# A routed mixture of experts behind a gated scan: how the first pages of tokens are cut and handed on

## The chip, the cores and the metric

The kernel runs on one core of one Trainium2 chip. The metric is the device time of one execution in microseconds. TensorE (PE in the profile, PEld its weight loads) does the matmuls, VectorE (DVE) and ScalarE (ACT) the elementwise work, GpSimd (POOL) starts the scatters, and SyncE (SP) starts the loads.

## The reference

There are 4 sequences of 5056 steps with 256 channels. A gated linear scan runs along each; its 20224 outputs are tokens. Each token goes to the one of 8 experts with the largest logit, passes two layers of that expert, and is scaled by its gate.

```python
for t in range(S):
    h = a_t[:, t] * h + x_gated[:, t]
    y[:, t] = h
...
logits = x @ w_gate + modality_bias[modality_id]
e_idx = np.argmax(logits, axis=1)
...
for e in range(E):
    mask = e_idx == e
    h = np.maximum(x[mask] @ w1[e], 0.0)
    out[mask] = gate_w[mask, None] * (h @ w2[e])
```

The gate's logits are small beside the bias of the token's modality, and there are two modalities, drawn at random. So nearly all tokens go to two experts, which the kernel calls hot.

## The kernel before, in words

**Chunks.** The steps are cut into 23 chunks: four of 128 steps (512 tokens over the 4 sequences), seventeen of 256 (1024 tokens), one of 128 and one of 64. For each chunk the kernel loads its inputs (`load_chunk`), runs the scan on VectorE (`scan_chunk`), scales and splits the result into two halves of 16 bits (`size_chunk`, `split_chunk`), routes it (`route_chunk`) and scatters its rows to a list in memory (`rows_part`, `scatter`, L813). In the list each expert has a region of its own of NCAP rows; a token's place is the expert's region plus its running count. `route_chunk` keeps the running counts in `be`, and those of the two hot experts, in units of 256 rows, in a small tile `b2` for each chunk (L800).

**Pages.** Work for TensorE comes in pages: that many consecutive rows of one expert's region. `choose_pages` runs along with everything else, and `choose_two` makes a pair, one page of each hot expert. It writes the first rows of the two pages to a tile `sel` (L917), which SyncE reads into a register before it loads the rows (`load_rows`: a transposing load of X at L1091, and the gates `mt` at L1092). `u` holds how far each hot expert has been handed on. The size of a pair is fixed when the program is built, while the counts are known only on the chip. So a pair is handed on when the tokens routed so far, less a margin `behind` for each hot expert, cover all that was chosen plus the new pair. If an expert has fewer rows than the page needs, its `sel` is set to `NULLS`, a page of null rows whose outputs go nowhere, and `u` stays.

The first pair has 128 rows per page, the next ones 256, and after the weights' block sums are ready (`block_sums`) pairs of 512 (`WIDE`), whose first layer takes 14 groups of products instead of 16. When all is routed, one pair of 256 that need not be full ends the hot list.

**Cold pages.** What is left goes to pages of 128 of whichever expert has most left (`choose_cold`). Such a page loads that expert's two weights, 1 MB each, through four buffers `wr` (`cold_weights`), scales and converts them into halves on ScalarE and VectorE (L297, L347, L350, L353) and then runs as other pages do. One is chosen for the experts that are not hot, one at the very end for any. Then `over` is the largest count still left (L984). If it is 1 or more, a block of instructions behind a branch (`more_pages`, L1401) chooses and runs two more such pages, and inside it a further branch does the same with six, and so on.

**Order.** A planner in the kernel's own code (`run`) decides the order of the instructions on each engine when the program is built: each thread yields an engine, a duration and a condition, and the earliest, or of near ones the most urgent, is issued. `mark`, `room` and `give` are its due times and buffers. `drained(n)` is the time at which TensorE has begun pages of n rows in all; `look` holds choices back to 384 rows ahead of that, or 2944 once the block sums are there. On the chip the engines follow the order and wait for each other by semaphores only.

TensorE interleaves a page's first layer (L1166, or L1256 for pages of 512) with the second layer of the page before (L1326). A page's hidden values pass ScalarE and VectorE (L1103, L1105), its outputs ScalarE (L1117), and a scatter on GpSimd (L1121) puts 128 rows at a time into the result.

Of the kernel before, what the change touches and what calls it, by code (L numbers as in the profile page):

```python
# [9 lines left out]
F32 = mybir.dt.float32  # L10
# [4 lines left out]
ALU = mybir.AluOpType  # L15
AX = mybir.AxisListType

P = 128
B, S, D, E, FF = 4, 5056, 256, 8, 1024
# [3 lines left out]
WIDE = 512  # L23
NCAP = N + 256
NULLS = E * NCAP
# [4 lines left out]
CHUNKS = [(128 * k, 128) for k in range(4)] + [(512 + 256 * k, 256) for k in range(17)] + [(4864, 128), (4992, 64)]  # L30
# [4 lines left out]
HOT = 2  # L35
# [11 lines left out]
C_STEP = 2  # L47
URGENT = 0.5
HURRY = 5
ROW_STEP = 2.4  # L50
LAG = 3.0


def behind(n):

    return 1.2 * n ** 0.5 + 8


def columns(c):
# [18 lines left out]
def kernel(  # L78
# [13 lines left out]
    nc = tc.nc  # L92
    pool = lambda name, bufs, **k: ctx.enter_context(tc.tile_pool(name=name, bufs=bufs, **k))
    const = pool("const", 1)
    pa = pool("pa", 2)
    sm = pool("sm", 2)
# [30 lines left out]
    for e in range(E):  # L127
# [23 lines left out]
        out=cmp, in0=rank.rearrange("p e o -> p o e").broadcast_to(one8), in1=ids.broadcast_to(one8), op=ALU.is_equal  # L151
# [7 lines left out]

    u = const.tile([1, HOT], F32, name="u")  # L160
    nc.vector.tensor_scalar(out=u, in0=key[:, 0:HOT, 0], scalar1=NCAP / 256.0, scalar2=None, op0=ALU.mult)
    cold = const.tile([1, E], F32, name="cold")
    nc.vector.tensor_scalar(out=cold, in0=ev, scalar1=HOT - 0.5, scalar2=8.0, op0=ALU.is_ge, op1=ALU.mult)

# [16 lines left out]
        out=um1, in_=um1, pattern=[[1, P]], base=0, channel_multiplier=-1,  # L181
# [33 lines left out]
    plan = {"end": 0.0}  # L215
# [4 lines left out]
    def room(tag, k=1):  # L220

        def at():
            d = slots[tag]
            old = [n - d.bufs for n in range(d.n, d.n + k) if n >= d.bufs]
            return max((d.back.get(n, FAR) for n in old), default=0.0)
        return at
# [8 lines left out]
    def allof(*fs):  # L235
        def at():
            t = 0.0
            for f in fs:
                t = max(t, f())
                if t >= FAR:  # L240
                    break
            return t
        return at
# [446 lines left out]
    def rows_part(c, j):  # L690
# [34 lines left out]
        for u in range(k):  # L725
            yield "POOL", ROW_STEP if c > 7 else 1.3, None
            scatter(f"rows{c}", rt[:, u, 0:ROW], di[:, PART * j + u : PART * j + u + 1])
# [84 lines left out]
    def scatter(group, src, idx):  # L812
        ins = nc.gpsimd.indirect_dma_start(  # L813
            out=rows[:, :], out_offset=bass.IndirectOffsetOnAxis(ap=idx, axis=0),
            in_=src, in_offset=None, bounds_check=NULLS + WIDE - 1, oob_is_err=False,
        ).ins
        for gname in written:
            tc.declare_no_dep(ins, group=gname, reason="every token has a row of its own")
        tc.declare_no_dep(ins, group="loads", reason="a page's rows are written before it is chosen")
        if group not in written:  # L820
            written.append(group)
        puts.append((group, ins.name))
        tc.add_to_no_dep_group(group, ins)
        free["DMA"] = max(free["DMA"], plan["end"] - 1.3) + 0.37
        if "pe" in count:

            tc.add_manual_dep(
                ins, count["pe"], mybir.DependencyInfo(mybir.DependencyClass.Sync, mybir.DependencyReason.DATA)
            )
# [7 lines left out]
    def null_rows():  # L837

        for k in range(2):
# [3 lines left out]
            for e in range(E):  # L843
                yield "POOL", ROW_STEP, None
                scatter("rows_null", nt, ni[:, e : e + 1])
# [13 lines left out]
    pages, queue = [], []  # L859
    count = {"chosen": 0, "ended": False, "cold": 0, "rows": 0}  # L860
# [3 lines left out]
    def routed(t=FAR):  # L864
        n = 0
        while n < NC and all(mark.get(("put", n, j), FAR) <= t for j in range(parts(n))):
            n += 1
        return n

    def enough():  # L870

        at, have = 0.0, 0
        want = count["chosen"] + HOT * (256 if pages else P)
        for c in range(NC):
            at = max([at] + [mark.get(("put", c, j), FAR) for j in range(parts(c))])
            if at >= FAR:
                return FAR
            have += B * CHUNKS[c][1]
            if have - HOT * behind(have) >= want:
                return at  # L880
        return at

# [20 lines left out]
        if not left:  # L903
            give("sel", ticket)

    def choose_two(size, full):

        sel, ticket = new_sel()
        b2 = tiles["b2", routed(plan["end"]) - 1]
        z = size / 256  # L910
        if full:
            d = sm.tile([1, HOT], F32, name=f"d{len(pages)}", tag="d2")
            nc.vector.tensor_tensor(out=d, in0=b2, in1=u, op=ALU.subtract)
            yield "DVE", 0.08, None, 0.0
            nc.vector.tensor_scalar(out=d, in0=d, scalar1=z, scalar2=float(NULLS), op0=ALU.is_lt, op1=ALU.mult)
            yield "DVE", 0.08, None, 0.0
            nc.vector.scalar_tensor_tensor(out=sel, in0=u, scalar=256.0, in1=d, op0=ALU.mult, op1=ALU.max)  # L917
            first = plan["end"]
            yield "DVE", 0.08, None, 0.0
            if z == 1:  # L920
                nc.vector.scalar_tensor_tensor(out=u, in0=d, scalar=0.0, in1=u, op0=ALU.is_equal, op1=ALU.add)
            else:
                nc.vector.tensor_scalar(out=d, in0=d, scalar1=0.0, scalar2=z, op0=ALU.is_equal, op1=ALU.mult)
                yield "DVE", 0.08, None, 0.0
                nc.vector.tensor_tensor(out=u, in0=u, in1=d, op=ALU.add)
        else:
            nc.vector.tensor_scalar(out=sel, in0=u, scalar1=256.0, scalar2=None, op0=ALU.mult)
            yield "DVE", 0.08, None, 0.0
            nc.vector.scalar_tensor_tensor(out=u, in0=u, scalar=z, in1=b2, op0=ALU.add, op1=ALU.min)
        left = [0] * HOT  # L930
        for e in range(HOT):
            pg = new_page(size, e, sel, e, not full)
            pg.ticket = ticket, left
            queue_page(pg)
        count["chosen"] += HOT * size
# [51 lines left out]
    def choose_pages():  # L987
        other, at = None, FAR
        summed = lambda: max(mark.get(("sw", e), FAR) for e in range(HOT))
        look = lambda: drained(count["chosen"] - (LOOK if summed() >= FAR else LOOK_END))()  # L990
        while True:
            yield "DVE", 0.08, allof(enough, room("sel"), look)
            if other is None and routed(plan["end"]) == NC:

                add(null_rows(), (0, 5), plan["end"])
                other, at = (yield from choose_cold(True)), len(pages) + 2 * HOT
                add(cold_weights(other), (1, 3), plan["end"])
                yield "DVE", 0.08, room("sel")
            if len(pages) >= at:
                queue_page(other)  # L1000
                at = FAR
            have = sum(B * t for _, t in CHUNKS[: routed(plan["end"])])
            size = 256 if pages else P
            if summed() <= plan["end"] and have - HOT * behind(have) >= count["chosen"] + HOT * WIDE:
                size = WIDE
            if have - HOT * behind(have) < count["chosen"] + HOT * size:
                break
            yield from choose_two(size, True)
        yield "DVE", 0.08, allof(room("sel"), look, seen("null"))
        yield from choose_two(256, False)  # L1010
        if at < FAR:
            queue_page(other)

        t = sm.tile([1, HOT, E], F32, name="thot", tag="thot", bufs=1)
        yield "DVE", 0.08, None, 0.0
        for r in range(HOT):
            nc.vector.tensor_scalar(out=t[:, r], in0=hm[:, r], scalar1=u[:, r : r + 1], scalar2=65536.0, op0=ALU.mult, op1=ALU.mult)
        for r in range(HOT):
            nc.vector.tensor_tensor(out=tk, in0=tk, in1=t[:, r], op=ALU.max)

        yield "DVE", 0.08, room("sel")
        last = yield from choose_cold(False)
        queue_page(last)
        add(cold_weights(last), (1, 3), plan["end"])
        tiles["over"] = over()
        count["ended"] = True
# [342 lines left out]
    def start_chunk(c):  # L1369
        at = PRIO.get(c, (9 + C_STEP * c, 10 + C_STEP * c, 11 + C_STEP * c, 10 + C_STEP * c))  # L1370
        add(load_chunk(c), (0, 10 + C_STEP * c))
        add(scan_chunk(c), (0, at[2]), urgent=c < HURRY)
        add(size_chunk(c), (0, at[2]), urgent=c < HURRY)
        add(split_chunk(c), (0, at[1]), urgent=c < HURRY)
        add(route_chunk(c), (0, at[0]), urgent=c < HURRY)
        for j in range(parts(c)):
            add(rows_part(c, j), (1, at[3]), urgent=c < HURRY)

# [83 lines left out]
```

## Time and profile before

| what | value |
|---|---|
| median of three runs | 951.44 us (950.36 to 954.1) |
| the profiled execution | 952.39 us, of which the span of the profile is 950.5 us |
| mean granted TensorE clock | 0.978 |
| PE busy | 869.7 us, 91% of the span |
| DVE, ACT, POOL busy | 700.0, 671.6, 484.7 us |
| moved by the DMA queues | 160.43 MB, mean 169 GB/s |

The page gives busy time for each engine, then the span in 40 equal slices with the busy share in tenths, the granted clock and the DMA share. A row of a group names the line, engine, operation, what it writes and reads, how many, the busy time and mean, and after the bar the idle time ahead of it with what ended it. A row of a timeline begins with the start and the length in us. A row of a stage has its bounds, its length, then for each engine the busy time with the number of instructions, the granted clock, the DMA share and GB/s.

### The profile page before, as it was taken

How to read it: one execution, taken by the hardware profiler on the slowest of the kernel's cores; microseconds unless marked ns; L12 is line 12 of the kernel's file. 1: busy time of each engine (PE TensorE's matmuls, PEld its weight loads, DVE VectorE, ACT ScalarE, POOL GpSimd, SP SyncE). 2: the span in 40 equal slices, each digit the busy share in tenths (PEclk: the TensorE clock that was granted, in tenths of full speed). 3: DMA queues.
4: the chain of work that ended last, by engine and by line, in shares of the span. 5: the costliest groups of instructions: out<-in, count | busy, mean ns of one | idle time of the engine just before them, and what ended most of it. 6: DMA issues, size and time to landing. Idle time of an engine off the chain costs nothing.

```text
span 950.5 us, 22224 instructions
## 1 busy us (share of the span) xinstructions
PE 869.7 (91%) x8462; PEld 775.0 (82%) x8462; DVE 700.0 (74%) x1535; ACT 671.6 (71%) x960; POOL 484.7 (51%) x506
## 2 busy tenths in 40 slices
PE   2268995879999999999999999999999999999996
PEld 1256884769898888888888888988888888888886
DVE  4977785788888877799886888976886666645551
ACT  6876795866898778889578789844765555554742
POOL 5232456367876758857776658745544221222122
PEclk9988997989999999999999999999999999999999
DMA  8746896759999799987788988685733322213410
GB/s 292 230 150 175 223 244 166 223 135 221 267 203 228 226 256 232 265 224 195 185 217 185 274 208 214 163 161 119 184 79 85 57 62 51 52 45 68 131 36 24
DMA packets 222759, 160.43 MB, mean 169 GB/s; under 512 B 197297, under 2 KB 201522, under 8 KB 216114
## 3 DMA queue, kind: packets, MB, share of 16 engines
q1 hardware_dynamic: 205714, 114.49, 51.2%
q0 software_dynamic: 16224, 44.25, 14.2%
q8 instruction: 68, 1.11, 0.5%
q14 instruction: 49, 0.40, 0.1%
q10 hardware_dynamic: 704, 0.18, 0.1%
HBM read 72.96 MB, written 44.48 MB: 124 GB/s over the span
## 4 chain that ended last, share of the span: by engine, by line
PE 46%; issue 21%; DVE 11%; DMA 8%; POOL 7%; ACT 6%; POOLq 0%; SPq 0%; ACTq 0%; DVEq 0%
PE po L1326 21%; PE ph L1166 21%; POOL out_dram L1121 5%; DMA rows<-rt,di 3%; DVE x L546 3%; DVE H L1105 2%; DMA X<-rows 2%; DMA rt<-a 2%; POOL rows L813 1%; PE pb L1256 1%; DVE x L531 1%; ACT H L1103 1%; PE psl L679 1%; PE pa L1256 1%; DVE g L517 1%
## 5 line engine op out<-in xcount | busy, mean ns | idle before, releaser
L1166 PE MATMUL ph<-X,hw 128*128 128x256 f16 (+1 forms) x2688 | 332.1, 276 | 27.3 <-DMA X<-rows 27.3
L1326 PE MATMUL po<-hw,H 128*128 128x256 f16 x2640 | 328.1, 274 | 2.9 <-DVE H L1105 2.7
L1121 POOL DMA_INDIRECT out_dram<-ot,mt x160 | 195.3, 1221 | 259.7 <-ACT ot L1117 217.9
L813 POOL DMA_INDIRECT rows<-rt,di x158 | 229.4, 1452 | 173.3 <-issue 40.7
L1166 PEld LDWEIGHTS <-hw 128*128 128x128 f16 x2688 | 261.3, 100 | 59.5 <-DMA X<-rows 21.3
L1326 PEld LDWEIGHTS <-H 128*128 128x128 f16 x2688 | 259.5, 98 | 35.0 <-DVE H L1105 3.5
L1105 DVE SCALAR_TENSOR_TENSOR H<-ph,H 128x512 f16<-128x512 f32 (+1 forms) x232 | 151.8, 665 | 80.0 <-ACT H L1103 79.6
L1103 ACT ACTIVATE H<-ph 128x512 f16<-128x512 f32 (+1 forms) x232 | 133.2, 578 | 99.9 <-PE ph L1166 88.1
L1117 ACT ACTIVATE ot<-po,gt 128x256 f32<-128x256 f32 x160 | 75.2, 471 | 50.5 <-PE po L1326 43.5
L546 DVE TENSOR_TENSOR_SCAN x<-a,x 128x2048 f32<-128x2048 f32 (+2 forms) x23 | 88.1, 3829 | 0.8
L1326 PE MATMUL po<-hw,Hx 128*128 128x256 f16 x576 | 81.8, 273 | 0.1
L1326 PE MATMUL po<-hw,Hg 128*128 128x256 f16 x576 | 80.2, 273 | 0.0
L1326 PEld LDWEIGHTS <-Hx 128*128 128x128 f16 x576 | 56.2, 98 | 6.7 <-issue 0.3
L1326 PEld LDWEIGHTS <-Hg 128*128 128x128 f16 x576 | 56.4, 98 | 6.5
L1256 PEld LDWEIGHTS <-sw 128*128 128x128 f16 x576 | 56.4, 98 | 6.5
L531 DVE TENSOR_TENSOR x<-g,x 128x2048 f32<-128x2048 f32 (+2 forms) x23 | 45.8, 1991 | 15.8 <-ACT x L529 15.8
L663 ACT ACTIVATE a<-x,scy 128x1024 f16<-128x1024 f32 (+2 forms) x46 | 45.8, 1021 | 12.3 <-DVE scy L289 12.3
L666 DVE SCALAR_TENSOR_TENSOR a<-x,scy,a 128x1024 f16<-128x1024 f32 (+2 forms) x46 | 50.8, 1122 | 1.7 <-ACT a L663 1.7
L522 ACT ACTIVATE a<-a,ch 128x1024 f32<-128x1024 f32 (+2 forms) x46 | 50.7, 1118 | 0.0
L1103 ACT ACTIVATE Hg<-sv 128x512 f16<-128x512 f32 x48 | 30.0, 627 | 26.5 <-DVE sv L1204 26.2
L517 DVE SCALAR_TENSOR_TENSOR g<-g,x 128x2048 f32<-128x2048 f32 (+2 forms) x23 | 45.6, 1984 | 2.9 <-ACT g L513 2.9
L1199 ACT ACTIVATE sv<-pb 128x512 f32<-128x512 f32 x48 | 28.6, 595 | 25.9 <-PE pb L1256 24.3
(210 smaller groups left out, 1109.2 us busy)
## 6 DMA issues: line engine op xcount, KB each, us to landing
a<-in_r_gate_dram SPq DMA_DIRECT2D x17, 1024.0 KB
g<-in_i_gate_dram SPq DMA_DIRECT2D x17, 1024.0 KB
x<-in_x_dram SPq DMA_DIRECT2D x17, 1024.0 KB
wr<-in_moe_w_dram SPq DMA_DIRECT2D x4, 1024.0 KB
cr<-in_moe_w_dram SPq DMA_DIRECT2D x4, 1024.0 KB
a<-in_r_gate_dram SPq DMA_DIRECT2D x5, 512.0 KB
g<-in_i_gate_dram SPq DMA_DIRECT2D x5, 512.0 KB
x<-in_x_dram SPq DMA_DIRECT2D x5, 512.0 KB
```

Source lines behind the costliest of these rows:

```text
L517: nc.vector.scalar_tensor_tensor(out=g, in0=g, scalar=1.0, in1=x, op0=ALU.add, op1=ALU.mult)
L531: nc.vector.tensor_tensor(out=y, in0=g, in1=y, op=ALU.mult)
L546: nc.vector.tensor_tensor_scan(out=y, data0=a, data1=y, initial=0.0, op0=ALU.mult, op1=ALU.add)
L666: nc.vector.scalar_tensor_tensor(out=ys[:, 1, :, u, :], in0=yg[:, :, u, :], scalar=sc, in1=ys[:, 0, :, u, :], op0=ALU.mult, op1=ALU.subtract,)
L813: ins = nc.gpsimd.indirect_dma_start(out=rows[:, :], out_offset=bass.IndirectOffsetOnAxis(ap=idx, axis=0), in_=src, in_offset=None, bounds ...
L1103: nc.scalar.activation(hi, src, AF.Relu)
L1105: nc.vector.scalar_tensor_tensor(out=lo, in0=src, scalar=0.0, in1=hi, op0=ALU.max, op1=ALU.subtract)
L1117: nc.scalar.activation(ot, po, AF.Copy, scale=t.gt[:, a : a + 1])
L1121: ins = nc.gpsimd.indirect_dma_start(out=out[:, :], out_offset=bass.IndirectOffsetOnAxis(ap=t.mt[:, a, 0:1], axis=0), in_=ot, in_offset=No ...
L1166: ins = nc.tensor.matmul(ph[:, v, 0:st], lhsT, rhs, start=(m == 0 and v == 0), stop=(m == len(mm) - 1), skip_group_check=True,)
L1256: ins = nc.tensor.matmul(to[:, v, :], lhsT[s], rhs[x], start=(i in (1, 7) and v == 0 and m == 0), stop=(m == 2), skip_group_check=True,)
L1326: ins = nc.tensor.matmul(prev.po, prev.h(hx, f, rs_), wv[:, wx, f], start=(prev.count == 1), stop=(prev.count == 3 * NF))
```

## The change

The margin `behind` becomes 0 for the chunks 0 to 5 and stays as it was from chunk 6 on. The first pair has 256 rows per page like the following ones. While at most six chunks are routed, `choose_two` takes a new form: a page begins at `u`, or where fewer than 256 new rows are there, at 256 rows ahead of the count, so that it takes again rows that another page had; `u` then goes to the end of the page or to the count, whichever is lower. A null page remains for an expert that has fewer than 256 rows in all (`u0` is `u` at the start). At the end of the hot list, behind the pair of 256, stands a pair of 128.

```diff
+EARLY = 6
-def behind(n):
-    return 1.2 * n ** 0.5 + 8
+def behind(n, c):
+    return 1.2 * n ** 0.5 + 8 if c >= EARLY else 0
...
+    u0 = const.tile([1, HOT], F32, name="uo")
+    nc.vector.tensor_copy(u0, u)
...
-        want = count["chosen"] + HOT * (256 if pages else P)
+        want = count["chosen"] + HOT * 256
...
-            if have - HOT * behind(have) >= want:
+            if have - HOT * behind(have, c) >= want:
...
-    def choose_two(size, full):
+    def choose_two(size, full, again=False):
...
+        if again:
+            d = sm.tile([1, 4, HOT], F32, name=f"d{len(pages)}", tag="d2")
+            nc.vector.tensor_tensor(out=d[:, 0], in0=b2, in1=u0, op=ALU.subtract)
+            nc.vector.scalar_tensor_tensor(out=d[:, 1], in0=b2, scalar=-z, in1=u, op0=ALU.add, op1=ALU.min)
+            nc.vector.tensor_scalar(out=d[:, 2], in0=d[:, 0], scalar1=z, scalar2=float(NULLS), op0=ALU.is_lt, op1=ALU.mult)
+            nc.vector.scalar_tensor_tensor(out=sel, in0=d[:, 1], scalar=256.0, in1=d[:, 2], op0=ALU.mult, op1=ALU.max)
+            nc.vector.tensor_scalar(out=d[:, 3], in0=d[:, 0], scalar1=z, scalar2=z, op0=ALU.is_ge, op1=ALU.mult)
+            nc.vector.tensor_tensor(out=d[:, 3], in0=d[:, 3], in1=u, op=ALU.add)
+            nc.vector.tensor_tensor(out=u, in0=d[:, 3], in1=b2, op=ALU.min)
+        elif full:
...
-            size = 256 if pages else P
+            size = 256
...
-            yield from choose_two(size, True)
+            yield from choose_two(size, True, n <= EARLY)
         yield "DVE", 0.08, allof(room("sel"), look, seen("null"))
         yield from choose_two(256, False)
+        yield "DVE", 0.08, allof(room("sel"), look)
+        yield from choose_two(P, False)
```

More of the change, by code (lines that the diff above doesn't have):

```diff
@@ L910, in choose_two @@
         z = size / 256
-        if full:
+        if again:
+            d = sm.tile([1, 4, HOT], F32, name=f"d{len(pages)}", tag="d2")
+            nc.vector.tensor_tensor(out=d[:, 0], in0=b2, in1=u0, op=ALU.subtract)
+            yield "DVE", 0.16, None, 0.0
+            nc.vector.scalar_tensor_tensor(out=d[:, 1], in0=b2, scalar=-z, in1=u, op0=ALU.add, op1=ALU.min)
+            yield "DVE", 0.16, None, 0.0
+            nc.vector.tensor_scalar(out=d[:, 2], in0=d[:, 0], scalar1=z, scalar2=float(NULLS), op0=ALU.is_lt, op1=ALU.mult)
+            yield "DVE", 0.16, None, 0.0
+            nc.vector.scalar_tensor_tensor(out=sel, in0=d[:, 1], scalar=256.0, in1=d[:, 2], op0=ALU.mult, op1=ALU.max)
+            yield "DVE", 0.16, None, 0.0
+            nc.vector.tensor_scalar(out=d[:, 3], in0=d[:, 0], scalar1=z, scalar2=z, op0=ALU.is_ge, op1=ALU.mult)
+            yield "DVE", 0.16, None, 0.0
+            nc.vector.tensor_tensor(out=d[:, 3], in0=d[:, 3], in1=u, op=ALU.add)
+            yield "DVE", 0.16, None, 0.0
+            nc.vector.tensor_tensor(out=u, in0=d[:, 3], in1=b2, op=ALU.min)
+        elif full:
             d = sm.tile([1, HOT], F32, name=f"d{len(pages)}", tag="d2")
@@ L1001, in choose_pages @@
                 at = FAR
-            have = sum(B * t for _, t in CHUNKS[: routed(plan["end"])])
-            size = 256 if pages else P
-            if summed() <= plan["end"] and have - HOT * behind(have) >= count["chosen"] + HOT * WIDE:
+            n = routed(plan["end"])
+            have = sum(B * t for _, t in CHUNKS[:n])
+            size = 256
+            if summed() <= plan["end"] and have - HOT * behind(have, n - 1) >= count["chosen"] + HOT * WIDE:
                 size = WIDE
-            if have - HOT * behind(have) < count["chosen"] + HOT * size:
+            if have - HOT * behind(have, n - 1) < count["chosen"] + HOT * size:
                 break
-            yield from choose_two(size, True)
+            yield from choose_two(size, True, n <= EARLY)
         yield "DVE", 0.08, allof(room("sel"), look, seen("null"))
         yield from choose_two(256, False)
+        yield "DVE", 0.08, allof(room("sel"), look)
+        yield from choose_two(P, False)
         if at < FAR:
```

## The prediction

> **What bounds the kernel now.** I read the page's head and its slices first, then the busy time by stage, then the choices of pages on VectorE, the waits of TensorE, and the tail.
>
> ```profile
> span 950.5 us, 22224 instructions
> PE   2268995879999999999999999999999999999996
> 60.00:70.00 10.00, 3.15 (x36) 2.32 (x34) 7.69 (x20) 9.75 (x15) 7.80 (x7) 0.82 0.44 146
> 70.00:80.00 10.00, 5.79 (x32) 4.13 (x31) 4.79 (x19) 3.63 (x6) 0.00 (x0) 0.50 0.53 121
> 150.00:160.00 10.00, 1.14 (x11) 0.77 (x8) 5.34 (x11) 5.40 (x5) 8.23 (x9) 0.59 0.46 117
> 200.00:210.00 10.00, 3.65 (x32) 2.94 (x31) 8.75 (x32) 4.93 (x6) 6.37 (x6) 0.82 0.44 116
> 210.00:600.00 390.00, 387.91 (x3903) 347.44 (x3902) 318.27 (x662) 319.11 (x409) 275.81 (x227) 1.00 0.88 223
> 880.00:944.00 64.00, 62.88 (x601) 56.43 (x599) 30.29 (x55) 32.06 (x56) 13.39 (x14) 1.00 0.24 70
> PE ph L1166 <- DMA X<-rows: 27.3, 5, 8.9
> ```
>
> The stage rows give the length, then busy time of PE, PEld, DVE, ACT, POOL, then the granted clock. Up to 210 us TensorE runs out of pages: five waits for rows (27.3 us in all). From 210 us to 944 it is busy practically all the time. So there are two prices: work put into the early gaps is hidden, and work after 210 us is paid in full.
>
> ```profile
> 31.52 0.16 DVE L800 TENSOR_REDUCE b<-bh 1x2 f32<-1x16 f32 x1
> 41.58 0.19 DVE L913 TENSOR_TENSOR d<-b,u 1x2 f32<-1x2 f32 x1
> 57.61 0.16 DVE L800 TENSOR_REDUCE b<-bh 1x2 f32<-1x16 f32 x1
> 66.31 0.14 DVE L913 TENSOR_TENSOR d<-b,u 1x2 f32<-1x2 f32 x1
> L1121 POOL DMA_INDIRECT out_dram<-ot,mt x160 | 195.3, 1221 | 259.7 <-ACT ot L1117 217.9
> L1401 SPq TENSOR_LOAD <-over x1: 277/277/277, 902.8 to 902.8; - x1
> L1401 DVEq COMPARE_BRANCH  x1: 72/72/72, 940.0 to 940.0; - x1
> L1401 PEldq COMPARE_BRANCH  x1: 4194/4194/4194, 941.4 to 941.4; - x1
> 943.72 0.97 POOL L1121 DMA_INDIRECT out_dram<-ot,mt  x1 [1.70 <-ACT ot L1117]
> ```
>
> The first choice (41.58) comes after the counts of chunk 0 (31.52) and before those of chunk 1 (57.61): it sees 512 tokens. The 160 output scatters are 160 x 128 = 20480 rows: 20224 in hot pages and two cold pages of 128. So the block behind `over` (L1401) is jumped over today. Every engine reads `over` when its own stream gets there, SyncE at 902.8, VectorE only at 940.0: there is no common barrier, but a page chosen in that block is chosen after VectorE's main work.
>
> **What the data do.** The routing of the reference's inputs (counted from its own formulas) has two hot experts, 4 and 7:
>
> ```
> tokens routed   512  1024  1536  2048  3072  4096 ... 20224
> expert 4        267   527   783  1033  1567  2087 ... 10051
> expert 7        245   495   751  1008  1494  1998 ... 10124
> expert 2          0     2     2     7    11    11 ...    49
> ```
>
> Before: an expert's pages hold 128 + 38 x 256 + 256 = 10112 rows. Expert 7 leaves 10124 - 10112 = 12, which the last cold page takes; `over` is 0.
>
> After: at the first choice the size is 256, and expert 7 has 245 < 256. In the new code d[:,2] becomes NULLS, the page is a null page, d[:,3] adds 0, and `u` of expert 7 stays. A page can reach back over old rows only if the expert has 256 rows in all; here it has not. From then on expert 7 is one page behind: 495 counts suffice for its rows 0-255, 751 for 256-511, and so on; expert 4 is at or above half each time (267, 527, 783, 1033, 1567, 2087). No page overlaps, and no further one is null. At the end the pages hold 256 + 37 x 256 + 256 + 128 of expert 4 as before, but one page of 256 less of expert 7: 9856. 10124 - 9856 = 268 are left; the last cold page takes 128, `over` is 140, and the block runs with its two pages (128 and 12 rows). A further block would need a remainder above 256; there is none.
>
> **The change part by part.**
>
> *Margin 0 in the first six chunks and pages of 256.* Pages handed out after chunks 0 to 5 come to 512, 1024, 1536, 2048, 3072, 4096 rows instead of 256, 768, 1280, 1792, 2816, 3840. That is 256 more once, and these are expert 7's null page, so real rows stay the same.
>
> ```profile
> 74.24 2.74 PE L1166 MATMUL ph<-X,hw 128*128 128x256 f16 x12 [4.21 <-DMA X<-rows]
> 921.70 1.47 PE L1166 MATMUL ph<-X,hw 128*128 128x256 f16 x12
> 923.01 1.47 PE L1326 MATMUL po<-hw,H 128*128 128x256 f16 x12
> 936.14 0.83 PE L1166 MATMUL ph<-X,cw 128*128 128x128 f16 x12
> 936.81 1.47 PE L1326 MATMUL po<-hw,H 128*128 128x256 f16 x12
> ```
>
> Twelve matmuls take 1.31 us (921.70 to 923.01), or 0.67 with 128 columns (936.14 to 936.81). A page of 256 (48 + 48 matmuls) is 10.5 us, one of 128 (48 short, 24 long) 5.3, one of 512 (84 + 96) 19.7. The extra 256 rows (10.5 us) fall into 60 to 80 us, where PE idles 6.85 + 4.21 = 11.1 us: hidden on PE. Without that cover it costs 10.5.
>
> *PE from then on.* Before, 20224 - 256 = 19968 rows follow; after, 20224 - 512 = 19712, of which 256 are the pair of 128 at the end. With six pairs of 512 in both, this is 512 rows (21.0) less and one pair of 128 (10.6) more: -10.4 us. If the grid, now shifted by 256, gives five, two pairs of 256 (42.0) replace one of 512 (39.4): -7.8. The pages are paced by what PE has used, so after is one step ahead when the block sums are ready, and I take five: -7.8.
>
> *The new choice.* Seven small VectorE instructions instead of four or five, eight times: 23 more in all, at 0.19 us (their spacing in the rows at 785.04 below) 4.4 us on an engine 77% busy in 60 to 70. The null page adds four pairs of relu passes. Neither is shown in before, so bounds: 0 (VectorE idles half of 70 to 80) to 6 us at the last gap, 200 to 210. I take 1, nearest to the idle rows. The one copy at the start is 0.15, hidden behind the loads. The condition ahead of the last pair of 128 is one of the planner's, not a wait on the chip: it places the choice and, behind it in the same thread, the last cold page's. Before made that one at 785 for a page run at 932, so 0, at most 1.
>
> *The block at the end* is the large term. Its nearest rows are the cold pages of before:
>
> ```profile
> 785.04 0.15 DVE L940 TENSOR_TENSOR k<-be,tk 1x8 f32<-1x8 f32 x1
> 785.23 0.15 DVE L954 SCALAR_TENSOR_TENSOR k<-k,tieb 1x8 f32<-1x8 f32 x1
> 786.25 0.16 DVE L971 CAST sel<-sf 1x2 int32<-1x2 f32 x1
> L1086 SPq TENSOR_LOAD <-sel x2: 274/285/296, 886.8 to 890.3; - x2
> 886.42 0.38 SPq L384 DMA_DIRECT2D cr<-in_moe_w_dram  x1
> 889.87 0.37 SPq L384 DMA_DIRECT2D cr<-in_moe_w_dram  x1
> 890.00:891.00 1.00, 1.00 (x12) 0.90 (x10) 0.00 (x0) 0.21 (x2) 0.00 (x0) 1.00 0.99 370
> 672.00 0.94 SPq L384 DMA_DIRECT2D cr<-in_moe_w_dram  x2
> 680.33 1.91 ACT L297 ACTIVATE cw<-cr 128x2048 bf16<-128x2048 f32 x1
> 897.34 1.90 ACT L297 ACTIVATE cw<-cr 128x2048 bf16<-128x2048 f32 x1
> 899.80 0.28 PE L301 MATMUL ptc<-ssc,onesf 128*128 128x1 f32 x2
> 902.09 1.15 ACT L347 ACTIVATE cw<-cr,csc 128x1024 f16<-128x1024 f32 x1
> 903.27 1.28 DVE L353 SCALAR_TENSOR_TENSOR cw<-cr,csc,cw 128x1024 f16<-128x1024 f32 x1 [0.62 <-ACT cw L347]
> 912.96 0.74 DVE L350 TENSOR_SCALAR cw<-cr,csc 128x1024 f16<-128x1024 f32 x1
> 939.41 0.42 DVE L1105 SCALAR_TENSOR_TENSOR H<-ph,H 128x256 f16<-128x256 f32 x1 [1.56 <-ACT H L1103]
> 942.97 0.47 ACT L1117 ACTIVATE ot<-po,gt 128x256 f32<-128x256 f32 x1 [2.19 <-PE po L1326]
> ```
>
> First page, on before's clock from VectorE's branch at 940.0: choice 1.4 (785.04 to 786.41), 941.4. SyncE reads `sel`, issues rows, gates and weights: 3.1 (886.8 to 889.87) and 0.7 for the second read, 945.2. The first 1 MB lands after 4.4 to 8.3: 1.6 until bytes flow and 2.8 at 370 GB/s, or as at 672.00, when two landed by 680.33; I take 4.8 (little else is under way), 950.0. Square 2.1, sum on PE 0.75, scale 0.6: 953.5. Two halves by ScalarE 1.15 each, VectorE 1.28 behind each: 957.3. The second weight's square is free to start at 955.8; + 2.1 + 0.75 + 0.6 = 959.3; its conversion is all VectorE's, 2 x (0.74 + 1.28) = 4.0, 963.3. First-layer matmuls (2.7) lie beside that. Four relu passes of 0.42 and two small ones, 2.1; the last six matmuls 0.7; output 0.7: 966.8.
>
> Second page: its weights arrive under the first, but ScalarE does them after the first page's output; from the square on it takes the same 966.8 - 950.0 = 16.8: 983.6, and the scatter 1.2: 984.8. Before ended its last scatter at 943.72 + 0.97 = 944.7, and what follows (to 950.5, with the jump) stays. The block: +40.
>
> PE is cold in it. The row at 74.24 needed 2.74 for twelve matmuls after 4.2 us of idling, and full clock came at 81. First-layer matmuls of a page, at half clock throughout, take 5.4 instead of 2.7 and stick out by 1.4 from the 4.0 of conversion that cover them: 0 to 2.8 for the two pages; I take 1, since the row's half clock lasted 6 us. The Trainium skill, "TensorE: Matmul & The Clock Gate", Part 1, says the array's clock is halved after an idle window of about 3.4 us and released after about as long a busy one; by its 3.4 us a page's 48 matmuls would take 4.4, the two would stick out by 0.8 and the block stay at 41; at the trace's 6 us it would be 43 if nothing else hid it. This trace agrees with the halving (0.50), not with the length.
>
> Sum: -7.8 + 1 + 41 = +34 us. The profiled execution took 952.39 (span 950.5 and 1.9 around it), 0.95 above the median of 951.44; on the median it is 985.5, so 986.
>
> **The rivals.**
> 1. *The block stays jumped over; faster.* One mechanism: the last cold page holds 128, and expert 7's remainder is 12 plus the rows lost; it decides at 116 lost rows. If the first choice saw chunk 1's counts (495), expert 7 would lose only 50 to overlaps, `over` would be 0, and the time 951.4 - 7 = 944. Against it stand 41.58 and 57.61 and the same condition for that first choice in both codes. 4%.
> 2. *A cheaper block.* ScalarE squares the second page's weight as soon as it lands (about 963), and VectorE's passes overlap: block 30 to 35, time 974 to 979. For it: queues are separate. Against: ScalarE's stream is fixed when built, by a plan that asks for all four weight buffers first. 18%.
> 3. *A dearer block or no early cover.* Four weight buffers free only after the first page's second layer, loads of 8.3: another 8 to 10; or routing, with ScalarE 98% busy in 60 to 70, pays for the null page and main's -7.8 shrinks to nothing. 994 to 1006. 22%.
>
> **How the numbers follow.** Forecast (980 to 993) 50%, rivals 4, 18 and 22%, anything else 6%. 973 to 1003 leaves out the first rival and the far ends of the third, about 2 in 10 or less. Differences under 0.5% cannot be told from none here (three runs span 950.36 to 954.1). Faster 0.04, same 0.01, slower 0.95.
>
> **What would show it.** 162 output scatters and eight loads into `cr` instead of 160 and four; a stretch of some 40 us at the end with PE mostly idle at half clock; VectorE's L940 group behind the branch; 60 to 80 us fuller on PE; main's last ordinary page about 7 us earlier. The prediction is wrong if the scatters stay 160, or if the tail is there and main ends later than before.

## The result and the profile after

Four runs of the changed kernel have a median of 974.63 us (973.07 to 975.17) beside 952.20 us (950.36 to 954.10) of the kernel before: a ratio of 1.0233, interval 1.0208 to 1.0258. The profiled execution took 973.07 us with a span of 971.3, against 950.5 before: +20.8 us in the spans, where the prediction's sum was +34.

First the head of the page, the busy row of TensorE by slices, two groups, and the loads of cold weights, all of after (its lines stand some 22 lower than before: L1121 is now L1143, L1326 is L1348, L1166 is L1188, L1401 is L1423).

```profile
span 971.3 us, 22757 instructions
PE   2298997999999999999999999999999999999933
L1143 POOL DMA_INDIRECT out_dram<-ot,mt x162 | 209.2, 1291 | 288.1 <-ACT ot L1139 231.6
L1348 PE MATMUL po<-hw,Hx 128*128 128x256 f16 x480 | 68.4, 273 | 1.2 <-ACT ot L1139 0.7
cr<-in_moe_w_dram SPq DMA_DIRECT2D x8, 1024.0 KB
```

There are 162 scatters, eight cold loads and two poor slices at the end: the block that before jumped over has run with its two pages. The group on `Hx` (48 matmuls for each page of 512) has 480, ten pages, so five pairs of 512.

Next the stages of after that answer to those shown of before, with the tail, and TensorE's waits for rows between 30 and 300 us.

```profile
60.00:70.00 10.00, 8.44 (x88) 7.08 (x86) 8.62 (x26) 9.91 (x17) 5.07 (x4) 1.00 0.96 288
70.00:80.00 10.00, 8.67 (x83) 7.67 (x81) 9.06 (x27) 9.14 (x15) 4.74 (x7) 1.00 0.59 98
150.00:160.00 10.00, 8.98 (x56) 6.83 (x57) 2.07 (x3) 3.12 (x5) 3.02 (x5) 0.65 0.83 161
200.00:210.00 10.00, 9.38 (x111) 8.26 (x110) 8.56 (x23) 9.77 (x11) 7.99 (x7) 1.00 0.76 144
925.00:972.00 47.00, 17.00 (x152) 15.46 (x152) 18.00 (x38) 16.07 (x22) 2.53 (x3) 0.68 0.33 104
PE ph L1188 <- DMA X<-rows: 16.1, 5, 7.1
```

Between 60 and 80 us TensorE is now busy 17.1 us at full clock (8.9 us at clocks of 0.82 and 0.50 before): the null page lies in the gap. Between 200 and 210 it is busy 9.38 us instead of 3.65: that gap is gone too, which nothing in the prediction had said. In the tail it is busy 17 of 47 us, at a mean clock of 0.68.

Now the tail as a timeline: start, length, engine and line, and in brackets the idle time ahead with what ended it.

```profile
921.69 0.15 DVE L959 TENSOR_TENSOR k<-be,tk 1x8 f32<-1x8 f32 x1 [0.31 <-DVE H L1127]
924.61 0.97 POOL L1143 DMA_INDIRECT out_dram<-ot,mt  x1 [1.70 <-DVE dd L986]
927.21 0.39 SPq L387 DMA_DIRECT2D cr<-in_moe_w_dram  x1
930.59 14.69 SPq L387 DMA_DIRECT2D cr<-in_moe_w_dram  x3
932.36 1.91 ACT L300 ACTIVATE cw<-cr 128x2048 bf16<-128x2048 f32 x1 [8.03 <-DMA cr<-in_moe_w_dram]
940.07 5.28 PE L1188 MATMUL ph<-X,cw 128*128 128x128 f16 x48
940.71 0.75 DVE L353 TENSOR_SCALAR cw<-cr,csc 128x1024 f16<-128x1024 f32 x1
943.48 1.28 DVE L356 SCALAR_TENSOR_TENSOR cw<-cr,csc,cw 128x1024 f16<-128x1024 f32 x1
948.12 0.47 ACT L1139 ACTIVATE ot<-po,gt 128x256 f32<-128x256 f32 x1 [2.35 <-PE po L1348]
948.50 1.90 ACT L300 ACTIVATE cw<-cr 128x2048 bf16<-128x2048 f32 x1
955.98 4.32 PE L1188 MATMUL ph<-X,cw 128*128 128x128 f16 x48
963.76 0.47 ACT L1139 ACTIVATE ot<-po,gt 128x256 f32<-128x256 f32 x1 [3.04 <-PE po L1348]
964.50 0.97 POOL L1143 DMA_INDIRECT out_dram<-ot,mt  x1 [14.66 <-DVEq L1423]
```

The last scatter of the main part ends at 924.61 + 0.97 = 925.58, against 944.69 before; the last of all at 965.47. So the +20.8 us of the spans are a block of +39.9 and a main part that ends 19.1 us earlier (and what follows the last scatter is the same within 0.1). The block cost what the prediction said; the main part gained 12 us more than it said.

### The profile page after: what moved, and what is told of

It reads as the page before. It is cut to its first block, busy times and chain, and to the rows that moved or that the text cites. A ratio compares the mean times of both kernels' runs of the same rounds, so it can differ in the third digit from the quotient of the medians.

```text
span 971.3 us, 22757 instructions
## 1 busy us (share of the span) xinstructions
PE 883.2 (91%) x8636; PEld 787.6 (81%) x8636; DVE 712.0 (73%) x1600; ACT 677.9 (70%) x966; POOL 489.8 (50%) x508
## 5 line engine op out<-in xcount | busy, mean ns | idle before, releaser
L1188 PE MATMUL ph<-X,hw 128*128 128x256 f16 (+1 forms) x2880 | 351.3, 273 | 16.3 <-DMA X<-rows 16.1
L1143 POOL DMA_INDIRECT out_dram<-ot,mt x162 | 209.2, 1291 | 288.1 <-ACT ot L1139 231.6
L1348 PE MATMUL po<-hw,H 128*128 128x256 f16 x2832 | 350.0, 273 | 2.7 <-DVE H L1127 0.9
L1188 PEld LDWEIGHTS <-hw 128*128 128x128 f16 x2880 | 276.6, 98 | 51.9 <-DMA X<-rows 9.7
L1348 PEld LDWEIGHTS <-H 128*128 128x128 f16 x2928 | 282.1, 98 | 37.8 <-DVE H L1127 2.5
L1127 DVE SCALAR_TENSOR_TENSOR H<-ph,H 128x512 f16<-128x512 f32 (+1 forms) x256 | 165.1, 658 | 99.6 <-ACT H L1125 99.3
L1348 PE MATMUL po<-hw,Hx 128*128 128x256 f16 x480 | 68.4, 273 | 1.2 <-ACT ot L1139 0.7
L1348 PE MATMUL po<-hw,Hg 128*128 128x256 f16 x480 | 66.9, 273 | 0.0
L1348 PEld LDWEIGHTS <-Hx 128*128 128x128 f16 x480 | 46.8, 98 | 6.8 <-issue 1.5
L1348 PEld LDWEIGHTS <-Hg 128*128 128x128 f16 x480 | 47.0, 98 | 5.4
L563 ACT ACTIVATE g<-g 128x2048 f32<-128x2048 f32 (+2 forms) x23 | 38.2, 1661 | 6.3 <-DVE x L534 4.1
L528 ACT ACTIVATE x<-a 128x2048 f32<-128x2048 f32 (+2 forms) x23 | 38.5, 1672 | 4.4 <-issue 4.2
```

What stands on the lines that cost most here:

```text
L1127: nc.vector.scalar_tensor_tensor(out=lo, in0=src, scalar=0.0, in1=hi, op0=ALU.max, op1=ALU.subtract)
L1143: ins = nc.gpsimd.indirect_dma_start(out=out[:, :], out_offset=bass.IndirectOffsetOnAxis(ap=t.mt[:, a, 0:1], axis=0), in_=ot, in_offset=No ...
L1188: ins = nc.tensor.matmul(ph[:, v, 0:st], lhsT, rhs, start=(m == 0 and v == 0), stop=(m == len(mm) - 1), skip_group_check=True,)
L1348: ins = nc.tensor.matmul(prev.po, prev.h(hx, f, rs_), wv[:, wx, f], start=(prev.count == 1), stop=(prev.count == 3 * NF))
```

## The experiments

Each time is compared with runs of the kernel before taken with it on the same chip. The three groups below ran on three chips, on which the kernel before had medians of 952.94, 963.9 and 967.37 us; between groups only ratios are compared. The expectations of the first two groups give times on the scale of 952 us for the kernel before.

### The block alone, and the main part alone

`e1_jump` is the changed kernel with `over` set to 0:

```diff
+        nc.vector.tensor_scalar(out=k, in0=k, scalar1=0.0, scalar2=None, op0=ALU.mult)
         nc.vector.tensor_reduce(out=ov, in_=k, axis=AX.X, op=ALU.max)
```

> The changed kernel with its count of what is left multiplied by 0, so that the block behind the branch is jumped over; the last 140 rows of expert 7 are not computed. Theory (block +40 us, main part 19 us shorter): 974.6 - 40 = 934.6, between 932 and 938, main's last scatter ends near 925.6 as in the changed kernel. Rival (the block's price is nearer 30, some of it hidden behind main's end): 942 to 946.

Measured: 935.16 us (934.44 to 937.0), 0.9818 of the kernel before, interval 0.9795 to 0.9841. Without its block the changed kernel is 17.8 us faster than before, and 39.5 us faster than with it (974.63 - 935.16).

`e2_forced` is the kernel before with `over` raised by one, so that the block runs on null rows:

```diff
+        if count["cold"] == 2:
+            nc.vector.tensor_scalar(out=k, in0=k, scalar1=1.0, scalar2=None, op0=ALU.add)
```

> The kernel before with 1 added to its count of what is left, so that the block runs on two pages of null rows; every row is computed as before. Theory: the block costs 40 us wherever it stands, 952.2 + 40 = 992 (989 to 995). Rival (the block's price depends on the changed main part): 975 to 985.

Measured: 989.23 us (987.31 to 992.9), 1.0373, interval 1.0348 to 1.0399: +36.3 us in the medians. The end of its trace:

```profile
945.83 0.97 POOL L1123 DMA_INDIRECT out_dram<-ot,mt  x1 [1.70 <-DVE ko L940]
984.23 0.97 POOL L1123 DMA_INDIRECT out_dram<-ot,mt  x1 [14.83 <-ACT ot L1119]
```

From the main part's last scatter to the block's it is 38.4 us. Whichever kernel it stands in, and whether its rows are real or null, the block costs 36 to 40 us. That is shown from both sides, so the disputed part is the main one: where do 18 us come from, when the count of rows gave 7?

### First page, margin and end of the list apart

`e3_first128` is the changed kernel with a first pair of 128 again and no pair of 128 at the end, so no null page and no remainder of 268; margin 0 and the new choice stay.

```diff
-        want = count["chosen"] + HOT * 256
+        want = count["chosen"] + HOT * (256 if pages else P)
...
-            size = 256
+            size = 256 if pages else P
...
-        yield "DVE", 0.08, allof(room("sel"), look)
-        yield from choose_two(P, False)
```

> The changed kernel with a first pair of 128 and no pair of 128 at the end; margin 0 and the new form of choice are kept, so no null page, no remainder, the block is jumped over, and the rows handed on after each chunk are those of before. As built, the load of chunk 4's x stands between the rows of the second pair's two pages on SyncE (before: behind both). Theory (the order of the early loads carries some 11 us of the 19): 940 to 946. Rival (a page more of work in the early gaps carries them, by filling TensorE and keeping its clock): 950 to 954. Rival (the new choice in itself slows VectorE): 955 to 960.

Measured: 946.12 us (944.48 to 947.32), 0.9932, interval 0.9911 to 0.9953: 6.8 us faster than before, with the same pages in all and the gap at 60 to 80 still there. The time lies just above the theory's range. After each chunk it hands on as many rows as before, and its chunk 4 was counted at 132.89 and chunk 5 at 178.06 (130.14 and 179.04 before). So neither earlier rows nor an earlier count of these chunks made its gain; yet there was no wait for rows at 200 us.

`e4_margin` is the reverse: the kernel before with a first pair of 256 and a pair of 128 at the end, margin and old choice kept.

```diff
-        want = count["chosen"] + HOT * (256 if pages else P)
+        want = count["chosen"] + HOT * 256
...
-            size = 256 if pages else P
+            size = 256
...
         yield from choose_two(256, False)
+        yield "DVE", 0.08, allof(room("sel"), look)
+        yield from choose_two(P, False)
```

> The kernel before with a first pair of 256 and a pair of 128 at the end, margin and old form of choice kept: nothing is handed on before chunk 1, no null page. The load of chunk 4's x stays behind the second page's rows. Theory: the 256 rows done before chunk 1 are lost from the early gaps, 10.5 us less work done by 210 us: 958 to 964. Rival (pages of 256 from the start are what shortens main): 938 to 946.

Measured: 957.2 us (953.17 to 958.96), 1.0033, interval 1.0016 to 1.0049. A first pair of 256 that has to wait for its rows with the margin gains nothing; it is 0.3% slower. The rival, that the larger first pages alone are the gain, is out; the time lies just under the theory's range.

### One thing at a time

In these traces TensorE does its instructions in the order that the plan gave them. In before the rank matmul of chunk 5 (L775), on which the counts of that chunk and so the next pages hang, stands behind a page that itself waits for rows of chunk 4 (page 8). Rows of before, then of after:

```profile
158.98 8.21 PE L1166 MATMUL ph<-X,hw 128*128 128x256 f16 x60 [8.86 <-DMA X<-rows]
167.58 0.22 DVE L764 TENSOR_TENSOR oh<-ky,mx 128x64 f16<-128x64 f32 x1
176.69 0.19 PE L775 MATMUL psl<-oh,um 128*128 128x64 f16 x1
179.04 0.16 DVE L800 TENSOR_REDUCE b<-bh 1x2 f32<-1x16 f32 x1
```

```profile
143.15 0.22 DVE L767 TENSOR_TENSOR oh<-ky,mx 128x64 f16<-128x64 f32 x1
144.29 0.19 PE L778 MATMUL psl<-oh,um 128*128 128x64 f16 x1
145.36 0.16 DVE L803 TENSOR_REDUCE b<-bh 1x2 f32<-1x16 f32 x1
151.02 9.18 PE L1188 MATMUL ph<-X,hw 128*128 128x256 f16 x56 [6.49 <-DMA X<-rows]
```

In before the wait of 8.86 us holds the rank, and not on TensorE alone: the row at 167.58 (`oh` marks each token's expert) is VectorE's part of the same routing, and it stands behind that page's passes on VectorE, the last at 166.55. In after the rank is done 6.5 us ahead of the page that waits. Chunk 5 is counted at 145.36 instead of 179.04, and after has no wait for rows at 200 us. Whether that alone is the gain was tried with the planner's conditions, in the kernel before.

`e10_rank5`: page 8 may not be placed ahead of the counts of chunk 5.

```diff
-        ready = lambda: ready_at(cur)
+        ready = lambda: max(ready_at(cur), mark.get(("route", 5), FAR) if cur.n == "8" else 0.0)
```

> The kernel before with one more condition for the planner: page 8 may begin only once chunk 5 is routed. The order on TensorE changes at one place: chunk 5's rank matmuls (L775) stand ahead of page 8's first layer, which waits for its rows until 159, instead of behind 60 of its matmuls. Nothing else is in it: no page of 256 at first, no margin 0. Theory (a rank held behind a page that waits for rows is what cost before its third gap): chunk 5 routed some 15 to 20 us earlier, the gap at 200 to 210 closes, 942 to 946. Rival (load order of chunk 4's x, or the filler, is the cause): 951 to 954.

Measured: 962.33 us, 0.9981, interval 0.9947 to 1.0016. The theory fell on the time (942 to 946 would be a ratio of 0.989 to 0.993), though its mechanism happened:

```profile
159.16 0.16 DVE L800 TENSOR_REDUCE b<-bh 1x2 f32<-1x16 f32 x1
200.00:210.00 10.00, 9.49 (x112) 8.50 (x111) 9.54 (x21) 8.05 (x10) 7.03 (x5) 1.00 0.90 282
240.00:300.00 60.00, 54.98 (x519) 47.61 (x517) 45.23 (x91) 45.03 (x60) 35.81 (x29) 0.97 0.83 226
```

Chunk 5 is counted 20 us earlier and the gap at 200 is closed, but TensorE now idles 5 us between 240 and 300, where the trace of before has it busy for all 60 (before has no trace on this chip). 3.2 us of that are short stops for which the profile shows no wait ("issue"); the traces of before and of the first group have none of them (last section), so they need not come from the plan.

`e6_load` is the kernel before with the inputs of chunk 4 loaded ahead of the second pair's rows (chunk 4 counted at 118.19 instead of 130.14); `e7_late` is the changed kernel with that load held back behind them (126.65 instead of 119.63).

```diff
-        add(load_chunk(c), (0, 10 + C_STEP * c))
+        add(load_chunk(c), (0, 1 if c == 4 else 10 + C_STEP * c))
```

```diff
+            late = [seen(("issued", 3))] if (c, name) == (4, "x") else []
-            yield "DMA", 2.9 * z, room(tag), -9.0
+            yield "DMA", 2.9 * z, allof(room(tag), *late), -9.0
...
+                mark["issued", pg.n] = plan["end"] - 2.0
```

> The kernel before with the load of chunk 4 made urgent in the planner, so that its x is issued ahead of the rows of the second pair as in the changed kernel. The ranks of chunks 2 and 3 now stand ahead of the pages that wait for rows, chunk 5's still behind page 8. Theory of the held rank: chunks 2 to 4 are routed earlier by some 4 to 8 us, chunk 5 stays late: 946 to 952. Rival (the load alone is the cause): 938 to 943.

> The changed kernel with the load of chunk 4's x put behind the rows of the second pair, as in before; in the plan chunk 5's rank then falls behind page 8 again. The block runs as in the changed kernel. Theory: the 10 us come back, 982 to 987. Rival (the null page as filler is what shortens main): 973 to 977.

Measured: `e6_load` 962.92 us, 0.9985, interval 0.995 to 1.0019; `e7_late`, block included, 980.25 us, 1.0158, interval 1.0085 to 1.0232. The early load alone gives nothing to be measured, and the changed kernel without it is no slower (1.0233 with it, in the result above); the expected loss of 10 us did not come. Load order is not what carries the gain by itself.

`e7_late` says more. As its expectation has it, the rank of chunk 5 stands behind the waiting page again:

```profile
153.51 8.16 PE L1190 MATMUL ph<-X,hw 128*128 128x256 f16 x60 [6.96 <-DMA X<-rows]
168.51 0.26 PE L779 MATMUL psl<-oh,um 128*128 128x64 f16 x1
169.65 0.16 DVE L804 TENSOR_REDUCE b<-bh 1x2 f32<-1x16 f32 x1
```

Chunk 5 is counted 24 us later than in after (169.65 for 145.36), and by the ratios nothing of the gain is lost. In `e3_first128`, `e6_load` and `e7_late` the wait for rows at 200 us is gone too, with chunk 5 counted at 178.06, 175.41 and 169.65. So the changed kernel's gain needs neither the early load nor the early rank, and the gap at 200 closes without the early rank.

`e5_filler` is the kernel before with one null page of 256 queued behind its first pair, which counts as handed on:

```diff
...
             yield from choose_two(size, True)
+            if "null" not in count:
...
+                sel, ticket = new_sel()
+                nc.vector.tensor_scalar(out=sel, in0=u, scalar1=0.0, scalar2=float(NULLS), op0=ALU.mult, op1=ALU.add)
+                pg = new_page(256, 1, sel, 1, False)
...
+                queue_page(pg)
+                count["null"] = 256
+                count["chosen"] += 256
```

> The kernel before with one null page of 256 rows more, queued behind the first pair of 128, which no expert loses: everything else (margin, choice, sizes, end) as before, no remainder, the block jumped over. Chunk 5's rank stands behind the page that follows chunk 4. Rival (filler): TensorE is kept busy and at full clock in the first gap, 938 to 944. Theory: the filler is only hidden and the third gap stays, 950 to 955.

Measured: 959.39 us, 0.9935, interval 0.9902 to 0.9968. A page that computes nothing of use, 10.5 us of TensorE's work, makes the kernel before some 4 to 6 us faster. That lies between the rival's 938 to 944 (0.984 to 0.991) and the theory's 950 to 955 (0.997 to 1.002). But the gaps did not vanish, one grew. Its waits at the starts of pages:

```profile
77.94 2.74 PE L1176 MATMUL ph<-X,hw 128*128 128x256 f16 x12 [4.85 <-DMA X<-rows]
159.73 8.03 PE L1176 MATMUL ph<-X,hw 128*128 128x256 f16 x60 [12.51 <-DMA X<-rows]
202.47 1.48 PE L1176 MATMUL ph<-X,hw 128*128 128x256 f16 x12 [0.73 <-DMA X<-rows]
```

### Together

What is gained in one gap may be taken back in the next, so the last group put the parts together, with the changed kernel without its block beside them (`f0_jump`, the edit of `e1_jump`).

> The changed kernel with the block at the end jumped over once more (140 rows of one expert are not computed), as the reference for the three other kernels on this chip. Every theory: 0.980 to 0.984 of the kernel before, about 17 us less.

Measured: 951.18 us, 0.9858, interval 0.9816 to 0.99: a little less of a gain than the expected 0.980 to 0.984 and than on the first chip, intervals overlapping.

`f4_fillload` is `e5_filler` with the edit of `e6_load`; `f5_fillloadrank` adds the condition of `e10_rank5`, for page 9, since the null page shifts the numbers by one.

> The kernel before with one null page of 256 behind its first pair and with the load of chunk 4 ahead of the rows of the second pair. All rows computed. The null page alone gave 0.9935 of the kernel before, the early load alone 0.9985. Theory that the gaps have to close together (the one gap that is left takes back what another gives): the wait of 12.5 us for rows of chunk 4 at about 160, which the null page alone left, shrinks to 7 us or less, and the time falls to 0.982 to 0.989. Rival (load order is worth nothing, with the filler or without): 0.991 to 0.995.

> f4_fillload with the ranks of chunk 5 ahead of the page that waits for rows of chunk 4 (in TensorE's order the ranks stand before page 9's first layer). All rows computed. Theory that the gaps have to close together: 0 to 4 us less than f4_fillload, at best that of f0_jump plus the null page's extra work. Rival: the same as f4_fillload within 1 us, since no wait for rows is left behind 200.

Measured: `f4_fillload` 957.52 us, 0.9905, interval 0.9873 to 0.9938; `f5_fillloadrank` 953.52 us (950.19 to 955.24), 0.9863, interval 0.9834 to 0.9891. Of `f4_fillload`, the wait near 155 and TensorE after 240; of `f5_fillloadrank`, the wait that stands in its place, the rank and the start of the page behind it, and the same stretch:

```profile
154.96 9.48 PE L1176 MATMUL ph<-X,hw 128*128 128x256 f16 x60 [9.42 <-DMA X<-rows]
240.00:300.00 60.00, 56.36 (x588) 49.36 (x586) 49.82 (x103) 51.52 (x65) 42.95 (x35) 1.00 0.79 213
```

```profile
155.94 0.35 PE L574 MATMUL psl<-ssy,onesb 128*128 128x1 bf16 x2 [10.22 <-ACT g L560]
156.15 0.21 PE L775 MATMUL psl<-oh,um 128*128 128x64 f16 x1
156.28 8.66 PE L1176 MATMUL ph<-X,hw 128*128 128x256 f16 x60
159.55 0.16 DVE L800 TENSOR_REDUCE b<-bh 1x2 f32<-1x16 f32 x1
240.00:300.00 60.00, 60.00 (x610) 53.95 (x608) 51.36 (x100) 55.58 (x71) 38.75 (x33) 1.00 0.97 246
```

The theory's 0.982 to 0.989 for `f4_fillload` was missed: its wait shrank from 12.5 to 9.4, not to 7, and its ratio lies between the theory's range and the rival's. The third part does not shorten TensorE's idle time there: it is 10.22 us, now ahead of a small matmul that waits for ScalarE (L560). What moved is the count of chunk 5, from 174.16 to 159.55. It brought 4.0 us in the medians (the two intervals overlap) and the full 60 us between 240 and 300; of the 3.6 us that `f4_fillload` idles in that stretch 2.5 are stops without a wait, so how much of the 4.0 is the plan's stays open. All three together, in a kernel that computes every row and has no block, reach 0.9863, the ratio of `f0_jump` within its interval, and the interval lies wholly below that of the null page alone (measured on another chip). The load and the rank, which alone gave 0.15 and 0.19%, gave 0.7 points of the ratio on top of the filler. `f5_fillloadrank` is faster than before by 1.4% and than the changed kernel by more; it is the best version run that computes everything.

`f1_skip` takes the null page's work away and leaves its place in the plan. It is `f0_jump` with the second page of the first pair left out on all engines, loads and order of the rest unchanged:

```diff
-                for m, (lhsT, rhs) in enumerate(mm):
+                for m, (lhsT, rhs) in enumerate(mm if pg.n != 1 else []):
```

and likewise for its second layer, relu passes, outputs and scatters.

> f0_jump with the second page of the first pair left out on TensorE, ScalarE, VectorE and GpSimd (48 + 48 matmuls, its relu passes and its two scatters; those 256 rows do not come out); the order of all other instructions and the loads is unchanged. Theory filler: the null page is worth something in itself because it keeps TensorE busy and its clock up; without it TensorE idles over 10 us before the rows of page 2 come, and pays about 3 us at half clock behind it (the first 6 us after 74.24 in the kernel before ran at 0.50), so 2 to 5 us slower than f0_jump. Theory order: the null page only moved other instructions ahead in the queues; the time is that of f0_jump within 1.5 us, or up to 3 us less, since VectorE and ScalarE have four relu pairs less.

Measured: 954.79 us (952.97 to 959.75), 0.9878, interval 0.9845 to 0.9911. Between 60 and 80 us, and the wait that closes the gap:

```profile
60.00:80.00 20.00, 11.20 (x74) 7.82 (x75) 14.53 (x47) 15.77 (x23) 8.96 (x10) 0.60 0.71 192
75.21 2.74 PE L1197 MATMUL ph<-X,hw 128*128 128x256 f16 x12 [4.01 <-DMA X<-rows]
```

The gap is back at half clock (in `f0_jump` it is 17.25 us of work at clock 1.00 and a wait of 0.81), and the median is 3.6 us up, as the filler theory said; but the intervals overlap, so that size isn't settled. Without any work in the null page the kernel is still 1.2% faster than before, 12.6 us in the medians. But like `f0_jump` it has one page of 256 real rows less in its main part than before, which the prediction's count puts at 7.8 us. That leaves about 5 us (0.8 to 7.2 by the interval) for the order of the plan.

## Why the prediction was right, and where it wasn't

**The data.** Right. The null page, the 268 rows left and `over` of 140 follow from the counts of the routing; the runs show what they led to, a block with two pages (162 scatters, eight cold loads) and no further one.

**The block.** Taken at 41, measured 39.9 by the traces and 39.5 by `e1_jump`. From the branch (about 921.5 us) to the end of the first page's output 27.1 us (948.59), predicted 26.8. The second page 15.6 us (948.59 to 964.23), predicted 16.8: the largest miss in it. The first load took 5.15 us to the start of its square (927.21 to 932.36) for 4.8. ScalarE did the second page's square right behind the first output (948.50), as was argued against the rival of a cheaper block. The rival of a dearer block was right that buffers hold the loads back: SyncE waited 11.8 us in all, two times, for VectorE's conversions of the first page (L356), and issued the last load only at 944.9. But its bytes were through by 951, and ScalarE took up that weight at 953.49 without a wait, so it cost nothing.

**The clock in the block.** The 48 first-layer matmuls took 5.28 and 4.32 us where 2.7 is the warm price and 5.4 was the bound; 4.05 of VectorE's conversion (940.71 to 943.48 + 1.28) covered most of it, and 1 us for both pages was enough. The Trainium skill, "TensorE: Matmul & The Clock Gate", Part 1, with its release after about 3.4 us of work, gives an estimate of 4.4 for such a page: the second page agrees, the first ran at half clock practically to its end.

**The null page.** Hidden, as predicted: 60 to 80 us took it up, and the waits for rows fell from 27.3 us to 16.1.

**Five pairs of 512.** Right (480 = 10 x 48).

**The main part's end** is the step that failed, the term "-7.8" with its "+1": it measured -19.1 in the traces and -17.8 in the medians. The prediction counted rows and their price and took all the other gaps as they were; for the changed order it allowed a cost of 0 to 6 us, at the gap of 200 to 210, and no gain. The gaps were not a property of the data: the plan is rebuilt around the new choices, and the gap at 200 to 210, which the prediction allowed to grow, closed. Of the profiled executions the sum was 986.6 (952.39 + 34.2) and 973.07 came: 13.5 us less, 12.3 of them in this term and 1.1 in the block. The chance of the main part's gain shrinking to nothing (third rival) was on the wrong side; a gain beyond -7.8 had no rival of its own. The measured 974.63 lies below the forecast's 980 to 993, in the second rival's 974 to 979; that is luck for the rival, since the block was not cheaper.

What the term left out can be read off the two traces. TensorE idles 75.0 us up to the last scatter of before (944.69 less 869.7 busy) and 59.4 us up to the main part's last in after (925.58 less 866.2, which is 883.2 without the block's 17.0). That is 15.6 us less; the null page was to fill some 10.4 of it, and the other 5 are idle time that the prediction took as given. TensorE's busy time fell by 3.5 us, where five pairs of 512 were to add 2.6. Most of this second difference of 6 us is the clock: between 60 and 80 us it was 0.82 and 0.50 before and 1.00 after. Estimated from windows of 1 us (busy time times one less the granted clock), the lower clock cost 10.0 us up to 925 us in before and 4.7 in after. So the null page was not only hidden: by this estimate its work also saved about 5 us of slow clock, a price that the prediction had put at nothing. `f1_skip`, 3.6 us slower in the medians without that work, points the same way, though its interval does not settle it.

How the 19 us divide is thus known in kind and not in all parts: about 7 by the prediction's count of rows, about 5 of clock, about 5 of idle time in a new order. `f5_fillloadrank` shows that a null page, the early load and the early rank together are worth 1.4% in a kernel that has all its rows in the main part; `e7_late` shows that the changed kernel does not owe its gain to the early load or the early rank. Which change of order closes the gap at 200, and why `e3_first128` gains 0.7% with chunks counted no earlier, stays open.

## What to carry to other kernels

Where engines follow a fixed order, an instruction that feeds later work is as late as the latest wait placed ahead of it on its engine. Look for such instructions, but do not take the wait for the price: freeing one alone measured as nothing here. Bound an order that will change from both sides, and price an idle gap with the lower clock behind it too. Try several closings together before calling each worthless. And when a padded page shifts what is left at the end, follow the remainder through to the last conditional block: 140 rows too many cost 40 us there.

## What the runs showed of the hardware

The three groups differ by more than the smaller effects here; each had its own chip and its own time, and the two were not separated. The kernel before had medians of 952.94, 963.9 and 967.37 us on the three chips, up to 1.5% apart. `e1_jump` and `f0_jump` are one and the same kernel, with spans of 933.0 us on the first chip and 948.5 on the third. Two stages of each, behind the early gaps:

```profile
210.00:240.00 30.00, 27.45 (x268) 23.54 (x265) 26.07 (x50) 25.09 (x33) 23.92 (x18) 0.94 0.85 210
240.00:600.00 360.00, 358.80 (x3656) 322.12 (x3655) 306.44 (x669) 299.32 (x394) 264.50 (x221) 1.00 0.88 225
```

```profile
210.00:240.00 30.00, 23.36 (x214) 19.16 (x212) 20.45 (x45) 21.52 (x27) 15.62 (x14) 0.89 0.66 150
240.00:600.00 360.00, 352.11 (x3573) 313.07 (x3570) 299.93 (x635) 292.91 (x383) 261.84 (x213) 1.00 0.87 219
```

On the third chip TensorE is busy 4.1 us less in the first stage and 6.7 in the second, where fewer bytes a second are moved (150 for 210 GB/s, 219 for 225). Most of what `f0_jump` idles more is put down to no wait at all. Of its rows of that kind between 30 and 900 us, 11.7 us in all, the two longest (us in all, times, longest):

```profile
PE psl L682 <- issue: 3.8, 6, 1.2
PE po L1349 <- issue: 3.5, 6, 1.2
```

`e1_jump` has no such row, nor have the traces of before, of the changed kernel and of the rest of the first group. All eight traces of the other two groups have them, 4.6 us (`f5_fillloadrank`) to 13.5 us (`f1_skip`) in all. So part of what `e10_rank5` lost again after 240 us may be the chip's and not the plan's; what stops TensorE there the profile does not show, and whether transfers are the cause or only follow wasn't tried.
